# A written-out cyclic order for the head pairs of an attention and feed-forward kernel

## Chip, cores and metric

The kernel runs on one core of a Trainium2 chip. The metric is the device time of one execution in microseconds; before the change the median of three runs is 488.45 us (487.97 to 488.66).

## What is computed

Attention with a bias that depends on positions, over batch 4, 8 heads, 576 positions, head size 64, and then a gated feed-forward layer with a convolution over positions (hidden size 1024):

```python
scores = scale * np.matmul(q, k.transpose(0, 1, 3, 2))
x = (psi_rel / psi_i)[..., None]
h = np.maximum(x @ w1 + b1, 0.0)
bias = h @ w2
scores = scores + bias.transpose(2, 0, 1)[None, :, :, :]
attn = np.exp(scores - np.max(scores, axis=-1, keepdims=True))
attn = attn / (np.sum(attn, axis=-1, keepdims=True) + 1e-09)
attn_out = np.matmul(attn, v)
x = attn_out.transpose(0, 2, 1, 3).reshape(B, S, H * D)
h = np.maximum(x @ w_in, 0.0)
conv_out = sum(conv_w[k] * hp[:, k:k + S, :] for k in range(3))
out = (h * sigmoid(conv_out)) @ w_out
```

## The kernel before

**Stages.** First the bias of all heads is computed and written to a DRAM tensor `bias_d`; then comes the attention; then the feed-forward layer, one batch entry after another. The change is about the attention.

**Pairs and units.** Two heads of one batch entry are a head pair. There are 16 (`seq`, pairs 0 to 15: four batch entries for each of four positions `p` of a pair among the heads). A pair's query rows are split into five units: unit 0 holds 64 rows of each of the two heads in one tile of 128 (the "short unit": one reduction, one exponent), units 1 to 4 hold 128 rows of each head, one head after the other.

**A unit's work.**
- `scores` (L371): TensorE multiplies queries and keys into a PSUM tile `s`; there are two such tiles (`psS`). Each product has two matmul instructions and each head two column halves. One instruction group of a unit has 8 matmuls.
- `reduce` (L382): VectorE adds the bias tile `bt`, writes the result to `sp` in SBUF and takes the row minimum. It frees the `s` tile. There are three `sp` tiles, used in turn.
- `expo` (L396): ScalarE takes the exponent in place and the row sum.
- `side_transposes` (L430) and `transposes` (L442): TensorE turns the result in pieces of 64 rows, the last 64 key columns into free columns of a score tile (the side), the rest into two of three PSUM tiles `tp`.
- copies (`act` L101 on ScalarE, `dve` L104 on VectorE) bring the turned pieces to `ptx` (units 0 to 2, 320 columns) and `pty` (units 3 and 4, 256 columns).
- `pv_parts` (L479): the value products, five parts for each of the two groups, into the one PSUM tile `o`; then ScalarE copies `o` to `x` (also L101).

**Sums.** `invert` (VectorE) takes the reciprocals of a pair's row sums, `sum_transposes` or the second half of `side_transposes` (L434) turns them, a copy brings them to `rt`, `store_sums` (L506, L507) writes them to a DRAM tensor, `spread_sums` (L512) loads them back to all partitions as `rb`, and `apply_norm` (L519) multiplies `x` by them on GpSimd.

**Weights.** The feed-forward weights come as 28 narrowing jobs: SP loads a piece (`load_w`), VectorE shifts (L110), ScalarE converts (L112), VectorE merges (L116), and GpSimd splits the result in two parts (L144, L145). Bias tiles of the next `p` are fetched by DMAs on GpSimd's queue (`load_bias`) in the pairs of the last batch entry.

**The order.** Each engine works through its instructions in the order of the program; waits are set by tiles. The attention is one loop over `flat`, the list of units. Round `u` issues the scores and reductions of unit `u + 2`, the side transposes of unit `u`, the exponents of unit `u + 1`, the main transposes and copies of unit `u`, and then some value products from the queue `fill`, by a fixed share:

```python
pv_share = (2, 2, 1, 3, 2)
```

A narrowing job starts in every second round, with one step after the transposes and one after the value products. The sums of pair `n - 1` are inverted, turned, stored and loaded during pair `n`, and pair `n - 2` is multiplied in the middle of pair `n`.

Of the kernel before, what the change touches and what calls it, by code (L numbers as in the profile page):

```python
# [19 lines left out]
def attention_ffn_kernel(  # L20
# [87 lines left out]
    def narrow_steps(w, u, raw):  # L108

        nc.vector.tensor_scalar(w, raw[:, :, 0], 29, None, op0=ALU.logical_shift_right)  # L110
        yield
# [36 lines left out]
    with tc.manual_schedule():  # L148
# [190 lines left out]
        def new_sp(n, t):  # L339
            tag = len(nms) % SPB  # L340
# [85 lines left out]
        def side_transposes(side, n, t, sums):  # L426

            spf = spt[n, t][0]
            for a, ra in enumerate(halves_):
                tr = nc.tensor.transpose(side[:, a, HS:HS + TL].bitcast(F32R), spf[ra, 8 * P:9 * P], identr[ra, ra])  # L430
                after_exp(tr, n, t)
            if sums is not None:
                for a, ra in enumerate(halves_):
                    nc.tensor.transpose(side[:, a, HS + TL:HS + P], rr_t[sums % 2][ra], ident[ra, ra])  # L434

        def transposes(n, t, side=None, sums=None):
# [8 lines left out]
            v3 = [x.rearrange("p (s x) -> p s x", x=TL) for x in ps]  # L445
            (d0, c0), (d1, c1) = (place(n, t, a if t else 0) for a in range(2))
            if t:
                dve(halves(d0[:, 8, c0:c0 + P]), side[:, :, HS:HS + TL])
                if sums is not None:
                    rts[sums] = r_p.tile([9, P], F32, name="rt")  # L450
                    dve(halves(rts[sums]), side[0:9, :, HS + TL:HS + P])
# [11 lines left out]
        def pv_parts(n, g):  # L463
            p, b = seq[n]
# [4 lines left out]
            def part(c):  # L469
# [13 lines left out]
                if c == 4:  # L483
                    del ptt[n, g]
                    waiting[n] -= 1
                    if b not in xb:
                        xb[b] = x_p.tile([P, NP, S], F32, name=f"x{b}", tag="x")
                    act(xb[b][:, p, x0:x0 + width], po[:, 0:width])

            return [lambda c=c: part(c) for c in range(5)]  # L490

# [24 lines left out]
        def apply_norm(n):  # L516
            p, b = seq[n]
            assert waiting[n] == 0
            nc.gpsimd.tensor_mul(xb[b][:, p], xb[b][:, p], rbs.pop(n))  # L519
# [90 lines left out]
        conv_weights = {68: load_conv, 71: narrow_conv, 73: turn_conv}  # L610
# [7 lines left out]
        NU = len(flat)  # L618
# [6 lines left out]
        def unit_steps(n, t):  # L625
# [10 lines left out]
            if t:  # L636
                side = psE.tile([P, 2, 512], F32, name="s")
                side_transposes(side, n, t, None)
            transposes(n, t, side)
# [48 lines left out]
        pv_share = (2, 2, 1, 3, 2)  # L688
        hs_ff = {}
        raw_w = {}  # L690
        job_steps = iter(())
# [3 lines left out]
        for u, (n, t) in enumerate(flat):  # L695
            p, b = seq[n]
            ui = units.index(t)
            sums = n - 1 if ui == (2 if n > 1 else 3) and n else None
            side = None
            if u + 2 < NU:  # L700
                for h in heads(flat[u + 2][1]):
                    if side is not None:
                        reduce(side, *flat[u + 2], 0)
                    side = scores(*flat[u + 2], h)
            if t:
                if side is None:
                    side = psS.tile([P, 2, 512], F32, name="s")
                side_transposes(side, n, t, sums)
            if u + 2 < NU:
                reduce(side, *flat[u + 2], h)  # L710
            if u + 1 < NU:
                for h in heads(flat[u + 1][1]):
                    expo(*flat[u + 1], h)
                turned_sp(*flat[u + 1])
            while fill and u == 5:
                fill.popleft()()
            transposes(n, t, side, sums)
            next(job_steps, None)

            parts = len(fill) if u < 5 else pv_share[ui]  # L720
            while fill and parts > 0:
                fill.popleft()()
                parts -= 1
            next(job_steps, None)
            del spt[n, t]
            if u + 2 >= NU:
                f = u + 2 - NU
                ffn_in(0, f)
            if u in (2, 4) or n > 1 and ui == 2 and n + 2 < NSEQ:
                load(n + 2 if n > 1 else 2 + u // 4)  # L730
            if u in conv_weights:
                conv_weights[u]()

            for at, do in ((u - 7, "load"), (u - 11, "split")):
                job = at // 2
                if at % 2 == 0 or not 0 <= job < 4 * KC + 2 * FE:
                    continue
                if job < 4 * KC:
                    src, dst = w_in[job // 4 * P:job // 4 * P + P], wi[job // 4]
                else:  # L740
                    src, dst = w_out[(job - 4 * KC) // 2 * P:(job - 4 * KC) // 2 * P + P], wo[(job - 4 * KC) // 2]
                cs = slice(job % 4 * 256, job % 4 * 256 + 256) if job < 4 * KC else slice(job % 2 * 256, job % 2 * 256 + 256)
                if do == "load":
                    raw_w[job] = (e_p if job % 3 else woe_p).tile([P, 256, 2], I32, name="raw_w", tag="h")
                    load_w(raw_w[job], src[:, cs])
                else:
# [262 lines left out]
```

## Time and profile before

| | |
|---|---|
| median of the runs | 488.45 us |
| the profiled execution's own time | 488.07 us |
| span in its profile | 486.3 us |
| TensorE, matmuls in flight | 470.2 us, 97% |
| TensorE, weight loads | 332.5 us, 68% |
| VectorE | 358.7 us, 74% |
| ScalarE | 301.9 us, 62% |
| GpSimd | 148.0 us, 30% |
| chain that ended last | TensorE 90%, ScalarE 4%, DMA 3% |

The span is from the first to the last instruction; the execution's own time is 1.8 us longer. A busy share is the union of an engine's instructions over the span. Matmuls are pipelined and their ends are modelled, so 97% does not say that TensorE is at its peak. The bias stage ends near 60 us, the attention near 291, the feed-forward layer fills the rest.

### The profile page before, as it was taken

How to read it: one execution, taken by the hardware profiler on the slowest of the kernel's cores; microseconds unless marked ns; L12 is line 12 of the kernel's file. 1: busy time of each engine (PE TensorE's matmuls, PEld its weight loads, DVE VectorE, ACT ScalarE, POOL GpSimd, SP SyncE). 2: the span in 40 equal slices, each digit the busy share in tenths (PEclk: the TensorE clock that was granted, in tenths of full speed). 3: DMA queues.
4: the chain of work that ended last, by engine and by line, in shares of the span. 5: the costliest groups of instructions: out<-in, count | busy, mean ns of one | idle time of the engine just before them, and what ended most of it. 6: DMA issues, size and time to landing. Idle time of an engine off the chain costs nothing.

```text
span 486.3 us, 10561 instructions
## 1 busy us (share of the span) xinstructions
PE 470.2 (97%) x3914; PEld 332.5 (68%) x3914; DVE 358.7 (74%) x876; ACT 301.9 (62%) x711; POOL 148.0 (30%) x221
## 2 busy tenths in 40 slices
PE   5978899999999999999999999999999999999996
PEld 3332366666666666666666668988888888888886
DVE  6999976788888889988887821594489238936971
ACT  6998886787777778777778722682264126424530
POOL 1000001354555725467267728006000600060000
PEclk9999999999999999999999999999999999999999
DMA  1899857588668796689952300000100200020003
GB/s 48 235 350 297 339 155 170 137 261 219 167 173 208 192 264 148 176 213 252 243 132 60 113 26 25 1 2 11 75 1 0 88 22 1 0 86 2 0 1 108
DMA packets 32582, 60.79 MB, mean 125 GB/s; under 512 B 7196, under 2 KB 15796, under 8 KB 32532
## 3 DMA queue, kind: packets, MB, share of 16 engines
q1 hardware_dynamic: 27380, 47.02, 34.3%
q0 software_dynamic: 4768, 12.77, 9.6%
q8 instruction: 31, 0.51, 0.4%
q10 hardware_dynamic: 384, 0.35, 0.2%
q14 instruction: 19, 0.16, 0.1%
HBM read 44.12 MB, written 15.98 MB: 124 GB/s over the span
## 4 chain that ended last, share of the span: by engine, by line
PE 90%; ACT 4%; DMA 3%; DVE 1%; issue 1%; DVEq 0%; SPq 0%
PE s L555 20%; PE o L479 18%; PE s L371 17%; PE tp L827 16%; PE tp L442 9%; PE o L827 4%; PE s L278 4%; DMA bias_d<-st 2%; ACT st L304 1%; ACT y L257 1%; PE s L430 1%; DVE sp L382 1%; ACT tl L304 1%; DMA bt<-bias_d 1%; DMA pars<-in_par_dram 1%
## 5 line engine op out<-in xcount | busy, mean ns | idle before, releaser
L382 DVE CUSTOM_DVE_ANT_0 sp<-s,bt 128x576 f32<-128x576 f32 x144 | 104.1, 754 | 33.3 <-PE s L371 20.9
L396 ACT ACTIVATE sp<-sp,nm 128x576 f32<-128x576 f32 x144 | 110.0, 768 | 0.0
L371 PE MATMUL s<-qk 64*128 64x288 f32 (+1 forms) x640 | 93.3, 431 | 3.4 <-DVE nm L382 2.6
L555 PE MATMUL s<-xs,wi 128*128 128x512 f32 x384 | 88.6, 390 | 0.0
L555 PEld LDWEIGHTS s<-xs,wi 128*128 128x128 f32 x384 | 71.8, 188 | 15.8 <-DVE pty L104 0.5
L371 PEld LDWEIGHTS s<-qk 64*128 64x128 f32 (+1 forms) x640 | 46.7, 175 | 45.3 <-DVE nm L382 14.9
L827 PE MATMUL tp<-wo,g 128*128 128x512 f32 x288 | 70.3, 389 | 0.0
L442 PE MATMUL tp<-identr,sr 64*128 64x64 f32 x1184 | 64.6, 248 | 1.4 <-ACT sp L396 1.4
L802 DVE SCALAR_TENSOR_TENSOR cv<-h,cw,cv 128x575 f32<-128x575 f32 x64 | 52.4, 818 | 16.7 <-ACT cv L797 14.8
L827 PEld LDWEIGHTS tp<-wo,g 128*128 128x128 f32 x288 | 54.0, 188 | 11.2
L442 PEld LDWEIGHTS tp<-identr,sr 64*128 64x128 f32 x1184 | 55.8, 136 | 7.6 <-ACT sp L396 2.1
L568 ACT ACTIVATE h<-s 128x512 f32<-128x512 f32 x32 | 19.1, 598 | 57.5 <-PE s L555 57.5
L261 DVE TENSOR_SCALAR y<-tl,inv,nb 128x576 f32<-128x576 f32 (+33 forms) x112 | 47.6, 499 | 0.0
L479 PE MATMUL o<-ptx,vt 128*64 128x320 f32 x300 | 46.8, 442 | 0.2 <-issue 0.2
L479 PE MATMUL o<-pty,vt 128*64 128x256 f32 x320 | 44.2, 393 | 0.0
L278 PE MATMUL s<-y,pars 128*32 128x512 f32 (+8 forms) x352 | 42.1, 500 | 1.8 <-DVE y L261 1.0
L144 POOL TENSOR_SCALAR xs<-x 128x512 fp32r<-128x512 f32 (+1 forms) x16 | 11.2, 701 | 105.5 <-DVE gt L822 105.5
L506 POOL DMA_DIRECT2D r_d<-rt x16 | 10.0, 627 | 87.2 <-DVE rt L104 87.2
L101 ACT ACTIVATE ptx<-tp 128x256 f32<-128x256 f32 (+1 forms) x64 | 26.7, 443 | 14.4 <-PE tp L442 14.2
L808 ACT ACTIVATE cv<-cv 128x576 f32<-128x576 f32 x32 | 21.9, 684 | 21.9 <-DVE cv L802 21.8
L809 DVE SCALAR_TENSOR_TENSOR cv<-cv,h 128x576 f32<-128x576 f32 x32 | 24.1, 753 | 14.0 <-ACT cv L808 14.0
L101 ACT ACTIVATE pty<-tp 128x512 f32<-128x512 f32 x32 | 19.0, 592 | 23.2 <-PE tp L442 23.2
(91 smaller groups left out, 646.3 us busy)
## 6 DMA issues: line engine op xcount, KB each, us to landing
qk<-in_qk_dram SPq DMA_DIRECT2D x32, 320.0 KB, 6.1
bias_d<-st SPq DMA_DIRECT2D x13, 607.0 KB, 6.0
bt<-bias_d POOLq DMA_DIRECT2D x24, 288.0 KB, 7.1
qk<-in_qk_dram SPq DMA_DIRECT2D x32, 144.0 KB, 6.2
rb<-r_d POOLq DMA_DIRECT2D x32, 144.0 KB, 3.1
vt<-in_v_dram SPq DMA_DIRECT2D x16, 256.0 KB, 7.1
raw_w<-in_moe_w_in_dram SPq DMA_DIRECT2D x16, 256.0 KB, 5.2
out_dram<-o SPq DMA_DIRECT2D x16, 256.0 KB, 2.0
```

The lines of the kernel that those rows point to most:

```text
L101: nc.scalar.activation(o, i, AF.Copy)
L261: nc.vector.tensor_scalar(y, dist[:, 0:n], inv[:, ig:ig + 1], nb1, op0=ALU.mult, op1=ALU.max)
L278: nc.tensor.matmul(ps[32 * j:32 * j + 32, a // 512 if n > 512 else blk % 2, 0:min(n - a, 512)], w2b, ys[j][:, a:min(n, a + 512)], start=Tr ...
L371: nc.tensor.matmul(ps[po, a, 0:HS], qt[rows, qo:qo + po.stop - po.start], qt[rows, KO + hh * HS:KO + hh * HS + HS], start=True, stop=True,)
L382: nc.vector.tensor_tensor_reduce(out=halves(spt[n, t][0][:, h]), in0=ps[:, :, 0:HS], in1=halves(bt[:, h]), op0=ALU.add, op1=ALU.min, scale ...
L396: exps[n, t, h] = nc.scalar.activation(sp[:, h], sp[:, h], AF.Exp, bias=nm[:, h:h + 1], scale=-1.0, accum_out=sms[n][:, col:col + 1],)
L442: tr = nc.tensor.transpose(ps[a][:, TL * s:TL * s + TL].bitcast(F32R), spf[ra, j:j + P], identr[ra, ra])
L479: nc.tensor.matmul(po[D * h:D * h + D, 0:width], vt[:, slot, :], pt[:, blk, :], start=(c == 0), stop=(c == 4),)
L555: nc.tensor.matmul(ps, wi[c][:, pw, f * P:f * P + P], rhs(c, px), start=(i == 0), stop=(i == 3 * KC - 1))
L802: nc.vector.scalar_tensor_tensor(out=cv[:, o:o + S - 1], in0=h[:, i:i + S - 1], scalar=cw[:, f, kk:kk + 1], in1=cv[:, o:o + S - 1], op0=AL ...
L809: nc.vector.scalar_tensor_tensor(out=cv, in0=cv, scalar=1.0, in1=h, op0=ALU.add, op1=ALU.mult)
L827: nc.tensor.matmul(ps, lhs(f, gi), wo[f][:, wj, cs], start=(f == 0 and i == 0), stop=(f == FC - 1 and i == 2),)
```

## The change

The loop over `flat` keeps only its first seven rounds (pairs 0 and 1). Pairs 2 to 15 run through a table `CYCLE` of operations, each with a unit, a pair relative to the current one, and an engine. The table's letters: `S` scores, `R` reduce, `E` exponent, `T` main transposes, `s` side transposes, `k0`, `k1`, `k0b`, `k1b`, `c` copies, `P` value product parts, `xb` the copy of `o`, `inv`, `sm`, `rt`, `st`, `sp`, `AN` the steps of the sums, `J1` to `J3` and `W` the steps of a narrowing job. The engine `A` or `V` of a copy is written in the table. `st` stands with the pair before the current one, `sp` with the one before that, `AN` with the third before.

`per_pair` gives the jobs of each pair; pairs 3, 7 and 11, which fetch bias tiles, have none. A job's load is issued three jobs ahead. The turn of the convolution weights moves from rounds 68 to 73 to rounds 1 to 6. Side transposes get their own columns of the latest score tile (`side_cols`).

```diff
@@
-        for u, (n, t) in enumerate(flat):
...
+        for u, (n, t) in enumerate(flat[:7]):
...
+            if u in (1, 4, 6):
+                (load_conv, narrow_conv, turn_conv)[u // 3]()
...
+        NJ = 4 * KC + 2 * FE
+        per_pair = [0, 0, 3, 0, 2, 3, 3, 0, 2, 3, 3, 0, 3, 2, 2, 2]
...
+        def job_step(j, k):
+            if k == 1:
+                _, dst, cs = job_slices(j)
+                jobs[j] = split_w_steps(e_p, dst[:, :, cs], raw_w.pop(j), ("cv", "cv"))
+            ins = next(jobs[j])
+            if k == 1 and j in first_job:
+                shifts[first_job[j]] = ins
+            if k == 2:
+                load_job(j + 3)
...
+        CYCLE = """
+            S:2,0,0:P S:2,1,0:P T:0,0:P inv:-1:V P:1,0,-1:P P:1,1,-1:P R:2,0,0:V E:1,0,0:A S:3,0,0:P E:1,1,0:A
...
+        """.split()
...
+        def side_cols():
+            if now[0] is None or used[0] + TL > 512:
+                now[0], used[0] = psS.tile([P, 2, 512], F32, name="s"), HS
+            used[0] += TL
+            return now[0][:, :, used[0] - TL:used[0]]
...
+            elif k == "AN":
+                mul = apply_norm(n)
+                if shifts:
+                    tc.add_manual_dep(mul.ins, shifts.pop(max(shifts)).ins.name, DATA)
+                if n == NSEQ - B:
+                    x_parts(0, NP - 1)
...
+        for m in range(1, NSEQ + 1):
+            if m == NSEQ:
+                ffn_in(0, 1)
+            for entry in CYCLE:
...
+                if at[-1] == NSEQ:
+                    instead(op)
+                elif at[-1] < NSEQ and (at[-1] > 1 or op in late) and op not in begun and op not in tail:
+                    emit(op, dve if eng == "V" else act)
+                    begun.add(op)
```

In the last pair `instead` puts feed-forward products where the next pair's scores would stand.

What the table makes of TensorE's order: the rows below are of the middle of the attention, before the change, from the scores of unit 2 of a pair to the value products of unit 2's round (L371 scores, L430 side transposes, L434 the sums, L442 main transposes, L479 value products; rows of one tile name are drawn together).

```order
L371 MATMUL s<-qk 128x288 x4
L442 MATMUL tp<-identr,sr_59 128x64 x10
L479 MATMUL o<-pty,vt_119 64x256 x4
L371 MATMUL s<-qk 128x288 x4
L430 MATMUL s<-identr,sr_60 128x64 x2
L442 MATMUL tp<-identr,sr_60 128x64 x16
L479 MATMUL o<-pty,vt_119 64x256 x4
L371 MATMUL s<-qk 128x288 x4
L430 MATMUL s<-identr,sr_58 128x64 x2
L434 MATMUL s<-ident,rr_161 128x64 x2
L442 MATMUL tp<-identr,sr_58 128x64 x16
L479 MATMUL o<-pty,vt_119 64x256 x2
```

The changed kernel at the same place, from the scores of unit 2 to those of the next pair's unit 0 (L370, L429, L434, L442, L483 are the same lines):

```order
L370 MATMUL s<-qk 128x288 x4
L442 MATMUL tp<-identr,sr_58 128x64 x10
L483 MATMUL o<-pty,vt_118 64x256 x4
L370 MATMUL s<-qk 128x288 x4
L442 MATMUL tp<-identr,sr_59 128x64 x16
L370 MATMUL s<-qk 128x288 x2
L429 MATMUL s<-identr,sr_59 128x64 x2
L370 MATMUL s<-qk 128x288 x2
L442 MATMUL tp<-identr,sr_60 128x64 x16
L434 MATMUL s<-ident,rr_160 128x64 x2
L429 MATMUL s<-identr,sr_60 128x64 x2
L370 MATMUL s<-qk 64x288 x4
```

Before, value products stand after the transposes of every unit. Now unit 1's main transposes are followed by scores, its side transposes stand between the two heads of unit 4's scores, and unit 2's transposes are followed by the next pair's unit 0. The value products of the second group stand in two blocks and those of the first in one block of five parts at the end of the cycle.

ScalarE before, from the copy of the 320 value columns of a pair (L101 copies, L396 exponents, L112 a narrowing step):

```order
L101 ACTIVATE x_938<-o 128x320
L396 ACTIVATE sp_57,sm<-sp_57,nm 128x576 x2
L101 ACTIVATE ptx<-tp 128x4x64
L101 ACTIVATE ptx<-tp 64x64
L112 ACTIVATE wu<-raw_w 128x256
L396 ACTIVATE sp_55,sm<-sp_55,nm 128x576 x2
L101 ACTIVATE ptx<-tp 128x8x64
```

And now, from the same copy to the first big copy of the next pair (L395 exponents, L111 a narrowing step):

```order
L101 ACTIVATE x_133<-o 128x320
L395 ACTIVATE sp_56,sm<-sp_56,nm 128x576 x2
L101 ACTIVATE ptx<-tp 64x64 x2
L395 ACTIVATE sp_57,sm<-sp_57,nm 128x576
L101 ACTIVATE ptx<-tp 128x4x64
L111 ACTIVATE wu<-raw_w 128x256
L395 ACTIVATE sp_57,sm<-sp_57,nm 128x576
L101 ACTIVATE ptx<-tp 128x8x64
```

The copy of the value columns stood in the middle of a pair's second round of value products; now it stands between the last work of one pair and the exponents of unit 1 of the next, and a second 64x64 copy has come from VectorE.

## Rows read from the trace of the kernel before

**Rows 1.** Windows, twelve pairs: PE, PEld, DVE, ACT, POOL busy; clock; DMA.

```profile
97.99:269.23 171.24, 171.24 (x1970) 113.26 (x1968) 147.62 (x430) 132.59 (x340) 95.10 (x149) 1.00 0.75 191
```

**Rows 2.** Timeline of PE, one pair: start, us, engine, line, what.

```profile
157.50 1.24 PE L371 MATMUL s<-qk 64*128 64x288 f32 x8
158.36 0.41 PE L430 MATMUL s<-identr,sr 64*128 64x64 f32 x2
...
159.35 1.08 PE L479 MATMUL o<-pty,vt 128*64 128x256 f32 x8
160.36 1.24 PE L371 MATMUL s<-qk 64*128 64x288 f32 x8
161.22 0.41 PE L430 MATMUL s<-identr,sr 64*128 64x64 f32 x2
...
162.28 0.65 PE L479 MATMUL o<-pty,vt 128*64 128x256 f32 x4
162.86 0.72 PE L371 MATMUL s<-qk 64*64 64x288 f32 x8
163.51 0.25 PE L430 MATMUL s<-identr,sr 64*128 64x64 f32 x2
...
171.75 0.51 PE L371 MATMUL s<-qk 64*128 64x288 f32 x2
```

**Rows 3.** Timeline of PE near the attention's start.

```profile
80.95 0.83 PE L442 MATMUL tp<-identr,sr 64*128 64x64 f32 x16
81.62 1.23 PE L371 MATMUL s<-qk 64*128 64x288 f32 x8
82.48 0.41 PE L430 MATMUL s<-identr,sr 64*128 64x64 f32 x2
...
83.37 0.75 PE L371 MATMUL s<-qk 64*128 64x288 f32 x4
```

**Rows 4.** Timeline of PE, a whole group of value products of 320 columns.

```profile
74.86 2.91 PE L479 MATMUL o<-ptx,vt 128*64 128x320 f32 x20
77.70 0.69 PE L371 MATMUL s<-qk 64*64 64x288 f32 x5
```

**Rows 5.** Timelines of PE, DVE and PEld: scores, reductions, a waiting weight load.

```profile
151.88 1.24 PE L371 MATMUL s<-qk 64*128 64x288 f32 x8
152.69 0.76 DVE L382 CUSTOM_DVE_ANT_0 sp<-s,bt 128x576 f32<-128x576 f32 x1 [1.12 <-PE s L371]
...
48.97 0.76 DVE L382 CUSTOM_DVE_ANT_0 sp<-s,bt 128x576 f32<-128x576 f32 x1 [0.43 <-DMA bt<-bias_d]
49.65 0.08 DVE L382 DVE_READ_ACCUMULATOR2_ANT nm<- 128x1 f32 x1
...
49.78 0.30 PEld L371 LDWEIGHTS s<-qk 64*128 64x128 f32 x4 [2.51 <-DVE nm L382]
```

**Rows 6.** Timeline of ACT, back-to-back operations.

```profile
155.11 0.44 ACT L101 ACTIVATE x<-o 128x320 f32<-128x320 f32 x1 [0.68 <-PE o L479]
155.44 0.43 ACT L112 ACTIVATE wu<-raw_w 128x256 f32<-128x256 f32 x1
155.77 0.77 ACT L396 ACTIVATE sp<-sp,nm 128x576 f32<-128x576 f32 x1
...
156.53 0.76 ACT L396 ACTIVATE sp<-sp,nm 128x576 f32<-128x576 f32 x1
...
157.28 0.47 ACT L101 ACTIVATE ptx<-tp 128x256 f32<-128x256 f32 x2
```

**Rows 7.** Timelines of DVE and POOL: a first narrowing step, alone and beside GpSimd.

```profile
154.85 0.28 DVE L110 TENSOR_SCALAR wu<-raw_w 128x256 int32<-128x256 int32 x1
...
160.76 0.74 POOL L145 TENSOR_TENSOR wi<-wu,wi 128x256 fp32r<-128x256 f32 x1
160.89 0.76 DVE L110 TENSOR_SCALAR wu<-raw_w 128x256 int32<-128x256 int32 x1
```

More of the change, by code (lines that the diff above doesn't have):

```diff
@@ L484, in part, with pv_out @@
                     del ptt[n, g]
[L485 to L488, printed above, removed]
+                    if out:
+                        pv_out(n, g, act)
             return [lambda c=c: part(c) for c in range(5)]
+        def pv_out(n, g, copy):
+            p, b = seq[n]
+            x0, width = (XW, YW) if g else (0, XW)
+            waiting[n] -= 1
+            if b not in xb:
+                xb[b] = x_p.tile([P, NP, S], F32, name=f"x{b}", tag="x")
+            copy(xb[b][:, p, x0:x0 + width], ops_t.pop((n, g))[:, 0:width])
         def invert(n):
@@ L694, in attention_ffn_kernel @@
         wo = [wo01[:, f] for f in range(2)] + [woe_p.tile([P, 2, DM], F32R, name=f"wo{f}") for f in range(2, FE)]
-        for u, (n, t) in enumerate(flat):
-            p, b = seq[n]
-            ui = units.index(t)
-            sums = n - 1 if ui == (2 if n > 1 else 3) and n else None
+        for u, (n, t) in enumerate(flat[:7]):
+            sums = 0 if (n, t) == (1, 3) else None
             side = None
[L700 to L704, printed above, removed]
-            if t:
[L706 to L714, printed above, removed]
+            for h in heads(flat[u + 2][1]):
+                if side is not None:
+                    reduce(side, *flat[u + 2], 0)
+                side = scores(*flat[u + 2], h)
+            cols = [side[:, :, HS + i * TL:HS + i * TL + TL] for i in range(2)]
+            if t:
+                side_transposes(cols[0], n, t)
+            if sums is not None:
+                sum_transposes(cols[1], sums)
+            reduce(side, *flat[u + 2], h)
+            for h in heads(flat[u + 1][1]):
+                expo(*flat[u + 1], h)
+            turned_sp(*flat[u + 1])
@@ L715, in attention_ffn_kernel @@
             while fill and u == 5:
                 fill.popleft()()
[L717 to L721, printed above, removed]
+            place_all(transposes(n, t), n, t, cols[0], sums, cols[1])
+            while fill:
                 fill.popleft()()
-                parts -= 1
-            next(job_steps, None)
             del spt[n, t]
-            if u + 2 >= NU:
-                f = u + 2 - NU
-                ffn_in(0, f)
@@ L729, in attention_ffn_kernel @@
[L729 to L739, printed above, removed]
-                else:
[L741 to L746, printed above, removed]
-                    job_steps = split_w_steps(e_p, dst[:, :, cs], raw_w.pop(job), ("cv", "cv"))
@@ new lines, in attention_ffn_kernel @@
+        jobs, tiles, turned, side_of, sum_in, parts_of = {}, {}, {}, {}, {}, {}
+        now, used = [None], [0]
+        left, shifts = {}, {}
+        def job_step(j, k):
[7 more added lines that the diff above has]
+                load_job(j + 3)
@@ new lines, in after_turn, with instead @@
+        def after_turn(n, t):
+            if n == NSEQ - 2 and t > 1:
+                x_parts(0, t - 2)
+            if n == NSEQ - 1 and t in (1, 2):
+                load_wo(FE - 1 + t)
+        ahead = {}
+        def instead(op):
+            if op == ("S", 1, 0, NSEQ):
+                ahead[0] = psS.tile([P, 2, 512], F32, name="s")
+                main_products(ahead[0], 0, 0)
+            elif op[0] == "S":
+                now[0] = None
+            if op == ("E", 0, 0, NSEQ):
+                main_out(ahead[0], 0, 0)
```

174 lines of the change are left out of this document (126 added, 48 removed).

## The prediction

> **What bounds the kernel now.** I read the windows first. From 97.99 to 269.23 us, twelve head pairs, TensorE has a matmul in flight for 171.24 of 171.24 us at a granted clock of 1.00; VectorE is busy 147.62 and ScalarE 132.59 [rows 1]. Busy time alone proves little, since matmuls overlap, so the timeline of one pair comes next [rows 2]: the scores of one unit start at 157.50 and the same unit's of the next pair at 171.75, so a pair takes 14.25 us, and twelve take 171.24, or 14.27 each [rows 1]. No matmul row in between shows idle time in front of it. The starts within a pair show what fills it: TensorE goes round scores, transposes, value products once per unit, and each group takes a fixed time from its start to the next group's.
>
> The weight loads take 113.26 of the 171.24 us [rows 1], that is 66%. The Trainium skill ("Perfetto Trace Analysis", Identifying the Most-Contended Engine) calls matmul busy time a bad measure and judges TensorE's headroom by weight-load share; by that a third of the engine would be free and a wait elsewhere would set the pair. The trace bears this out only as rival 3 below: the same spacing pair after pair is what an engine limited by its own order looks like.
>
> **The price of a pair, by groups.** From start to next start, in the old order [rows 2]: scores of two heads 0.86 (157.50 to 158.36); side and main transposes, 18 instructions, 0.99 when value products follow; eight value products of 256 columns 1.01, four of them 0.58, so four more cost 0.43; 20 transposes 1.06; the scores of the short unit 0.65 (162.86 to 163.51). After scores, 18 transposes followed by scores instead of value products take 0.89 (82.48 to 83.37), and 16 transposes between value products and scores take 0.67 (80.95 to 81.62) [rows 3]: two transposes cost 0.083, and the step from transposes to scores is 0.10 cheaper than the step to value products. A whole group of 20 value products of 320 columns takes 2.84 (74.86 to 77.70) [rows 4], once instead of twice.
>
> **The change, part by part.** The matmuls are the same; the stops at value products fall from five in a pair to three. The new order, with those prices:
> scores of unit 2, 0.86; ten transposes of unit 0, 0.99 less four times 0.083, 0.66; eight value products 1.01; scores 0.86; 16 transposes followed by scores, 0.89 less 0.08, 0.81; scores of unit 4 with two side transposes between its heads; 20 transposes before the short unit, 1.06; the short unit 0.65; twelve value products 1.01 + 0.43 = 1.44; 16 transposes 0.67; scores 0.86; 20 transposes 1.06; the 20 value products 2.84.
> No row shows scores, two transposes, scores. It costs 0.86 if the two vanish behind the scores and 0.86 + 0.22 = 1.08 at most (0.22 is 0.89 less eight steps of 0.083); I take the middle, 0.97. Nor is there a row of transposes before the short unit: 0.96 if the step costs what it costs before scores, 1.06 as before value products; I take 1.06, since the short unit, like the value products, writes half of the partitions at a time. The short unit before value products is taken at its price before transposes.
> The sum is 13.75 us.
>
> **The new wait.** Only two score tiles exist, so the second head of unit 4 must wait until VectorE has reduced the second head of unit 3, with one group of transposes between instead of a whole unit. A reduction starts 0.81 after its scores group (151.88 to 152.69), the next one 0.68 later (48.97 to 49.65), and the weight load that was waiting comes 0.81 after the start of the reduction that frees its tile (48.97 to 49.78) [rows 5]. With unit 3's scores at 0.86 + 0.66 + 1.01 = 2.53, the reductions start at 3.34 and 4.02 and free their tiles at 4.15 and 4.83. Unit 4 wants them at 4.20 and about 4.80. The first is in time by 0.05; the second makes TensorE wait some 0.06 with the matmul's own start. So the pair takes **13.81**, and saves 14.25 - 13.81 = **0.44**.
>
> **The rest costs nothing while its cover holds.**
> - Copies change engines: the sums' copy and one big copy leave VectorE for ScalarE. VectorE is at 147.62 of 171.24 and gets lighter. ScalarE, 132.59 in twelve pairs, is 11.0 a pair and has 13.81.
> - ScalarE has one tight chain. The copy of the 320 value columns now stands ahead of the next pair's exponents, and waits for the last of the 20 value products: about 13.81 + 0.14, at 13.95. Behind it come four exponents, three small copies, a narrowing step and a big copy, which the transposes of unit 2 wait for, at 13.81 + 5.23 = 19.04. By the rows: the value copy 0.33 (155.11 to 155.44), the narrowing step 0.33, an exponent 0.76, two small copies 0.47 [rows 6]; in all 0.33 + 3.04 + 0.55 + 0.33 + 0.60 (a big copy, estimated from the small ones' rate) = 4.85, so 18.80, with 0.06 to release it 18.86. It is in time by some 0.2. Without the narrowing step it has 0.5.
> - The sums are stored, loaded and multiplied a pair or more later, so GpSimd's two waits on DMA get longer cover; nobody but the last multiplication is waited for.
> - 28 narrowing jobs stay 28; those moved out of the pairs that fetch bias tiles leave GpSimd's queue to the fetches there. Their loads stand three jobs ahead on SP's queue, behind the next pair's queries.
> - The turn of the convolution weights goes from the end of the attention to its start: the same transpose, no gain.
>
> **Sum.** Pairs 2 to 14 run whole cycles; the last pair has the same groups with feed-forward products in place of the next pair's scores, and I give it the same 0.44. 14 x 0.44 = 6.2. The profiled execution took 488.07 (its span is 486.3), so 481.9; the median of the runs, 488.45, stands 0.38 above it: **482.3**. The two open prices move it. With both cheap ends the wait of unit 4 still decides there, and only the 0.10 of the short unit is won: 13.71, 480.9. With the dear end of the split scores the wait vanishes in it: 13.86, 483.0.
>
> **Rivals.**
> 1. **GpSimd's port.** A first narrowing step took 0.28 alone (154.85), and 0.76 when it started beside a GpSimd subtraction of 0.74 (160.89 against 160.76) [rows 7]: 0.48 more. In the new order the second job of a pair starts just where the first job's split or the multiplication runs. VectorE has some 0.4 to spare before the last reduction of the cycle delays the next scores. If a job's step is held in most of the eleven pairs that have jobs, about 0.3 each remains on TensorE's path, 3.3 in all: 485.6. The Trainium skill ("SBUF — State Buffer", Who interferes with whom) has the shared port as an exclusive lock held for the whole instruction; this case's rows agree, and by that rule the multiplication, the longest of them, would hold a step longest.
> 2. **ScalarE becomes the bound: slower.** The chain above closes on itself: value products, value copy, four exponents, big copy, transposes of unit 2, value products. It decides once its eleven operations take 0.2 more. It loses what was won at 0.64 more, 0.06 an operation, and at 0.09 each (1.0) the pair takes 14.61, 0.36 over the old one: 14 x 0.36 = 5.0, 493.5. For it: no row has these operations back to back in this order. Against: each price above is from back-to-back rows.
> 3. **TensorE's order was not the bound**, or the savings are met by new waits of their size: 488.4. Against: the even spacing of [rows 2].
> 4. **The change gains more.** Both open prices are at their cheap ends and the reductions come early enough not to decide: 13.75 - 0.11 - 0.10 = 13.54, 0.71 a pair, 478.5; halfway from the forecast, 480.4. Against: VectorE's 0.81 and 0.68 are the same in every row I saw.
>
> **How the numbers follow.** Forecast (481 to 484) 0.52; rival 1 (484 to 487.4) 0.20; rival 4 0.11; rival 3 0.08; rival 2 0.09. A measurement of this kernel tells 0.2%, about 1 us, from no change. Faster is forecast, rivals 1 and 4: 0.83; same 0.08; slower 0.09. The range that leaves out rivals 2 and 3 and the far ends of the others is 479.8 to 486.8.
>
> **What would show it.** The scores of unit 2 should come every 13.8 us; eight value products, scores, 16 transposes, scores should stand in the timeline with the prices above; a weight load of the second head of unit 4 should show a short wait for VectorE. Wrong would be: a wait of transposes for ScalarE in each pair (rival 2), a narrowing step of 0.7 or more with scores waiting after it (rival 1), or the groups' prices themselves, if a step from transposes to scores costs as much as one through value products.

## The result, and the profile after

The changed kernel took **483.12 us** (median of 4, 482.75 to 485.34) beside 488.56 us of the kernel before in the same comparison: 0.99 of its time, 95% interval 0.9869 to 0.9932. The forecast was 482.3, so the gain is there and 0.8 us of it are missing in the medians. The profiled execution took 483.41 us; the prediction's sum for it was 481.9, so 1.5 us are missing there.

The page of the changed kernel: its first line, busy time by engine, and the chain that ended last, by engine.

```profile
span 481.5 us, 10562 instructions
PE 464.8 (97%) x3914; PEld 333.7 (69%) x3914; DVE 347.4 (72%) x834; ACT 312.9 (65%) x753; POOL 147.7 (31%) x221
...
PE 84%; DVE 7%; ACT 3%; DMA 3%; issue 1%; SPq 0%; DVEq 0%
```

As the copies moved, VectorE got 11.3 us lighter and ScalarE 11.0 us heavier. TensorE has 6 points less of the chain than before, and VectorE has 7% of it instead of 1%. Most of that is not the attention's: 21 us of VectorE's part lie before 66 us, 15 of them on L260 of the bias stage, where the chain took another path than before. From 98 to 250 us VectorE has none of the chain, in pairs 14 and 15 some 11 us: there are the new waits.

The windows, from the scores of unit 2 of pair 3 to those of pair 15, twelve pairs as in [rows 1] (columns as there).

```profile
97.99:264.59 166.60, 165.96 (x1970) 114.02 (x1968) 135.99 (x386) 140.26 (x371) 88.27 (x135) 1.00 0.74 189
```

The same 1970 matmuls take 166.60 us instead of 171.24, at the same granted clock of 1.00. They are no longer without a hole: 0.64 us have no matmul in flight.

The timeline of PE, one pair, to be read beside [rows 2].

```profile
97.99 1.24 PE L370 MATMUL s<-qk 64*128 64x288 f32 x8
98.85 0.72 PE L442 MATMUL tp<-identr,sr 64*128 64x64 f32 x10
99.50 1.08 PE L483 MATMUL o<-pty,vt 128*64 128x256 f32 x8
100.52 1.24 PE L370 MATMUL s<-qk 64*128 64x288 f32 x8
101.38 0.99 PE L442 MATMUL tp<-identr,sr 64*128 64x64 f32 x16
102.18 0.77 PE L370 MATMUL s<-qk 64*128 64x288 f32 x4
...
103.19 0.98 PE L442 MATMUL tp<-identr,sr 64*128 64x64 f32 x16
...
104.25 0.72 PE L370 MATMUL s<-qk 64*64 64x288 f32 x8
104.89 1.52 PE L483 MATMUL o<-pty,vt 128*64 128x256 f32 x12
106.34 0.83 PE L442 MATMUL tp<-identr,sr 64*128 64x64 f32 x16
107.01 1.24 PE L370 MATMUL s<-qk 64*128 64x288 f32 x8
...
108.95 2.91 PE L483 MATMUL o<-ptx,vt 128*64 128x320 f32 x20
111.79 0.51 PE L370 MATMUL s<-qk 64*128 64x288 f32 x2
```

From 97.99 to 111.79 a pair takes 13.80 us, and so do ten of the eleven from pair 3 to 13, within 0.02; pair 11 takes 13.89, because its short unit's scores come 0.08 late. **Pair 14 takes 14.65.** One more place is late: in pair 15, TensorE is at the end of the attention 21.30 us after the scores of unit 2 (264.59 to 285.90), before it was 21.45, a gain of 0.15 only. (In the two further traces of the changed kernel, below, pair 15 takes 21.00 and 21.01.)

The timelines of POOL, DVE and PE at the wait of pair 14.

```profile
258.54 1.42 POOL L529 TENSOR_TENSOR x<-x,rb 128x576 f32<-128x576 f32 x1
258.61 1.62 DVE L115 SCALAR_TENSOR_TENSOR wu<-wu 128x256 int32<-128x256 int32 x1
...
260.16 0.68 DVE L104 COPY ptx<-tp 128x512 f32<-128x512 f32 x1
...
260.89 0.34 PE L442 MATMUL tp<-identr,sr 64*128 64x64 f32 x4 [0.64 <-DVE ptx L104]
```

A last narrowing step takes 0.41 to 0.43 us in the pairs from 3 to 13. Here it starts 0.07 behind the start of GpSimd's multiplication by the inverted sums and takes 1.62. The copy of a transposed piece stands behind it on VectorE, and the transposes wait for the buffer that this copy frees: the 0.64 us without a matmul.

The same timelines at the wait of pair 15.

```profile
269.86 1.42 POOL L529 TENSOR_TENSOR x<-x,rb 128x576 f32<-128x576 f32 x1 [2.09 <-DVE wu L115]
270.50 0.93 DVE L110 TENSOR_SCALAR wu<-raw_w 128x256 int32<-128x256 int32 x1
...
272.23 0.68 DVE L104 COPY ptx<-tp 128x512 f32<-128x512 f32 x1
...
273.05 0.47 PE L442 MATMUL tp<-identr,sr 64*128 64x64 f32 x7 [0.50 <-DVE ptx L104]
```

Here it is a first narrowing step (0.29 alone), and the transposes wait 0.50. They also ask earlier than in a whole cycle: the last pair has no short unit of a next pair, 0.65 us of scores, in front of them.

**Where the time went.** The scores of unit 2 of pair 2 start 0.52 later than before (83.89 and 83.37). Of this 0.27 comes from the bias stage, which ended later in this execution (the same scores of pair 1 start at 66.44 and 66.17). The other 0.25 is the turn of the convolution weights, which now stands right in front of these scores. The timelines of PE at the turn, before and after.

```profile
274.63 0.24 PE L600 MATMUL tp<-ident,w 24*128 24x24 f32 x1
...
83.72 0.24 PE L610 MATMUL tp<-ident,w 24*128 24x24 f32 x1
```

With the turn between them, it is 0.91 from the transposes to the scores (82.98 to 83.89); without it, before, 0.65 (82.72 to 83.37). At its old place, in pair 15, the turn took 0.17 (274.63 to 274.80). Pair 2 gave 0.52 (14.62 to 14.10), pairs 3 to 14 gave 4.64 (171.24 to 166.60), pair 15 gave 0.15. Less the later start that is 4.79 at the first feed-forward product behind the attention (290.69 and 285.90), and still 4.79 at the start of TensorE's last matmul (482.16 and 477.37): the feed-forward layer passes it on whole. The two executions' own times differ by 4.66.

### The profile page after: what moved, and what is told of

The parts are those of the page before. It is cut to its first block, busy times and chain, and to the rows that moved or that the text cites. A ratio compares the mean times of both kernels' runs of the same rounds, so it can differ in the third digit from the quotient of the medians.

```text
span 481.5 us, 10562 instructions
## 1 busy us (share of the span) xinstructions
PE 464.8 (97%) x3914; PEld 333.7 (69%) x3914; DVE 347.4 (72%) x834; ACT 312.9 (65%) x753; POOL 147.7 (31%) x221
## 4 chain that ended last, share of the span: by engine, by line
PE 84%; DVE 7%; ACT 3%; DMA 3%; issue 1%; SPq 0%; DVEq 0%
PE s L565 21%; PE o L483 16%; PE tp L949 16%; PE s L370 15%; PE tp L442 9%; PE o L949 5%; DVE y L260 3%; DVE sp L381 2%; DMA bias_d<-st 2%; PE s L277 1%; ACT y L256 1%; ACT st L303 1%; DVE ptx L104 1%; DMA pars<-in_par_dram 1%; PE s L429 1%
## 5 line engine op out<-in xcount | busy, mean ns | idle before, releaser
L381 DVE CUSTOM_DVE_ANT_0 sp<-s,bt 128x576 f32<-128x576 f32 x144 | 105.5, 751 | 21.6 <-PE s L370 19.4
L395 ACT ACTIVATE sp<-sp,nm 128x576 f32<-128x576 f32 x144 | 110.4, 769 | 0.6 <-DVE nm L381 0.6
L370 PE MATMUL s<-qk 64*128 64x288 f32 (+1 forms) x640 | 94.9, 435 | 2.9 <-DVE nm L381 2.3
L442 PE MATMUL tp<-identr,sr 64*128 64x64 f32 x1184 | 69.3, 255 | 3.0 <-ACT sp L395 1.8
L442 PEld LDWEIGHTS tp<-identr,sr 64*128 64x128 f32 x1184 | 57.8, 136 | 17.4 <-ACT rt L101 3.8
L370 PEld LDWEIGHTS s<-qk 64*128 64x128 f32 (+1 forms) x640 | 45.7, 174 | 29.0 <-PE o L483 6.4
L260 DVE TENSOR_SCALAR y<-tl,inv,nb 128x576 f32<-128x576 f32 (+33 forms) x112 | 47.6, 500 | 0.0
L483 PE MATMUL o<-ptx,vt 128*64 128x320 f32 x300 | 43.7, 437 | 0.0
L483 PE MATMUL o<-pty,vt 128*64 128x256 f32 x320 | 41.2, 389 | 0.0
L101 ACT ACTIVATE pty<-tp 128x512 f32<-128x512 f32 x46 | 26.5, 595 | 19.4 <-PE tp L442 18.5
L277 PEld LDWEIGHTS s<-y,pars 128*32 128x32 f32 x352 | 15.5, 113 | 26.1 <-DVE y L260 11.4
```

The lines of the kernel that those rows point to most:

```text
L101: nc.scalar.activation(o, i, AF.Copy)
L260: nc.vector.tensor_scalar(y, dist[:, 0:n], inv[:, ig:ig + 1], nb1, op0=ALU.mult, op1=ALU.max)
L277: nc.tensor.matmul(ps[32 * j:32 * j + 32, a // 512 if n > 512 else blk % 2, 0:min(n - a, 512)], w2b, ys[j][:, a:min(n, a + 512)], start=Tr ...
L370: nc.tensor.matmul(ps[po, a, 0:HS], qt[rows, qo:qo + po.stop - po.start], qt[rows, KO + hh * HS:KO + hh * HS + HS], start=True, stop=True,)
L381: nc.vector.tensor_tensor_reduce(out=halves(spt[n, t][0][:, h]), in0=ps[:, :, 0:HS], in1=halves(bt[:, h]), op0=ALU.add, op1=ALU.min, scale ...
L395: exps[n, t, h] = nc.scalar.activation(sp[:, h], sp[:, h], AF.Exp, bias=nm[:, h:h + 1], scale=-1.0, accum_out=sms[n][:, col:col + 1],)
```

## The experiments

My theory: TensorE's order sets the time of a pair, by the prices of its groups; the rest is hidden. The main rival: it is hidden only where no narrowing step of VectorE meets an instruction of GpSimd.

**The changed kernel again**, twice.

> The changed kernel itself, again, as the base for the other runs of this chip. Theory (TensorE's order of groups) and rivals alike: 482.5 to 483.5 us, twelve of thirteen whole cycles of 13.80 to 13.81 us, one cycle (pair 14) of about 14.65.

> The changed kernel once more, to stand beside the kernel with the two edits in pairs 13 to 15: 482.8 to 483.6 us by either theory.

483.21 us (483.07 to 484.85), ratio 0.9899 (0.988 to 0.9918), and 483.56 us (482.7 to 483.96), ratio 0.9902 (0.9886 to 0.9919). Both traces have the cycles of the first one, with pair 14 at 14.62; pair 11 is at 13.92 in the first of them and at 13.81 in the second. Pair 15 takes 21.00 and 21.01 instead of 21.30: its first narrowing step beside the multiplication takes 0.63 there, not 0.93. So 0.3 of the wait of pair 15 belongs to the one execution shown above.

**Five stops at value products, all else of the change kept.** The table of the cycle is written in the order of the old rounds, with the new engines for the copies, the new places of the sums and the new pairs for the jobs.

```diff
-            S:2,0,0:P S:2,1,0:P T:0,0:P inv:-1:V P:1,0,-1:P P:1,1,-1:P R:2,0,0:V E:1,0,0:A S:3,0,0:P E:1,1,0:A
...
+            S:2,0,0:P R:2,0,0:V S:2,1,0:P R:2,1,0:V E:1,0,0:A E:1,1,0:A T:0,0:P k1b:0,0:A k0b:0,0:A k0:0,0:V k1:0,0:A
+            J1:0,0:V P:1,0,-1:P P:1,1,-1:P J2:0,0:A inv:-1:V
+            S:3,0,0:P R:3,0,0:V S:3,1,0:P s:1,0:P R:3,1,0:V E:2,0,0:A E:2,1,0:A T:1,0:P c:1,0:V k0:1,0:A k1:1,0:A
+            J3:0,0:V P:1,2,-1:P P:1,3,-1:P W:0,0:G
...
```

> The table is written in the old order of rounds, with five stops at value products, and keeps everything else of the change: copies on the engines of the new table, sums stored, loaded and multiplied as late, jobs in the same pairs. Theory (TensorE's order is the whole gain): 14.25 a pair, 488.5 to 489.5 us, as before the change. Rival (lighter VectorE and later sums carry it): 483 to 485.

488.51 us (487.74 to 489.91), ratio 1.0 (0.999 to 1.0011): the time before. The timeline of PE, the short unit of two pairs in a row.

```profile
106.76 0.72 PE L370 MATMUL s<-qk 64*64 64x288 f32 x8
...
121.01 0.72 PE L370 MATMUL s<-qk 64*64 64x288 f32 x8
```

14.25 us, as in [rows 2]. With the old order of TensorE's groups, moving copies, sums and jobs gains nothing. The gain is the order's. (VectorE's and ScalarE's orders stand in the same table and follow the rounds too.) Why a stop costs what it costs was not taken apart: the prices are measured, not explained.

**Four stops**: one of the two stops that the change takes out is put back.

```diff
-            k1b:0,0:A k0b:0,0:A R:2,1,0:V S:3,1,0:P J1:0,0:V k0:0,0:V E:2,1,0:A T:1,0:P R:3,0,0:V S:4,0,0:P
+            k1b:0,0:A k0b:0,0:A R:2,1,0:V S:3,1,0:P J1:0,0:V k0:0,0:V E:2,1,0:A T:1,0:P P:1,2,-1:P R:3,0,0:V S:4,0,0:P
...
-            T:2,0:P E:3,1,0:A J1:2,0:V sm:-1:P s:2,0:P E:3,0,0:A k1:1,0:A S:0,0,1:P E:4,0,0:A P:1,2,-1:P
+            T:2,0:P E:3,1,0:A J1:2,0:V sm:-1:P s:2,0:P E:3,0,0:A k1:1,0:A S:0,0,1:P E:4,0,0:A
```

> One part of the value products moves in the table from the second block to behind unit 1's transposes: TensorE stops at value products four times a pair instead of three; nothing else moves. Theory (the pair's time is the sum of TensorE's group prices): 16 transposes before value products 0.91, four value products 0.58, less 0.81 and less 0.43, so 0.25 more, less the 0.05 that unit 4 then need not wait: 14.0 a pair, 14 pairs, 2.8 us, 485.9 us. Rival (the gain came from VectorE's lighter load and the later sums): 483.1.

494.07 us (492.33 to 497.38), ratio 1.0121 (1.008 to 1.0162): slower than the kernel before, and far from the 485.9 that I expected. The cycles are 14.14 to 14.16 us in some pairs, 0.15 above the 14.0 that the prices of groups give, and 14.98 or 14.99 in six (4, 5, 8, 9, 12 and 13). The timelines of POOL, DVE and PE in one of the six.

```profile
119.34 1.40 POOL L529 TENSOR_TENSOR x<-x,rb 128x576 f32<-128x576 f32 x1
119.53 1.37 DVE L110 TENSOR_SCALAR wu<-raw_w 128x256 int32<-128x256 int32 x1
...
121.70 0.67 DVE L104 COPY ptx<-tp 128x512 f32<-128x512 f32 x1
...
122.52 0.30 PE L442 MATMUL tp<-identr,sr 64*128 64x64 f32 x3 [0.75 <-DVE ptx L104]
```

In the new order of three stops the second job's first step starts beside a split of 0.74 us and takes 0.68 (at 117.70 us); moved by a stop, it starts beside the multiplication and takes 1.37.

The six cycles make 5.0 us. The profiled execution (497.38 us) loses more in pair 15, which takes 25.78: there, too, steps are held, transposes wait 1.96 us for a copy of VectorE, and right behind that the granted clock is 0.50 from 285 to 290 us, the lower of its two levels (1.2 GHz). Twelve feed-forward products take 5.49 us there, and 3.04 in the changed kernel.

**Four stops, the multiplication held behind that step.** It already waits for the first step of a pair's first job; now it waits for that of the second.

```diff
-        first_job = {sum(per_pair[0:n]): n for n in range(NSEQ) if per_pair[n]}
+        first_job = {sum(per_pair[0:n]) + 1: n for n in range(NSEQ) if per_pair[n]}
```

> The four-stop order of the last batch again, and the multiplication by the inverted sums on GpSimd now waits for the first step of the pair's second narrowing job instead of that of the first job; nothing else is moved. Theory (GpSimd's port): the 0.83 us that six of the four-stop cycles took beyond 14.15 us came from that step standing beside the multiplication (1.37 us, alone 0.29). It then falls back to 0.29 to 0.4 us, the six cycles to 14.15, and the run from 494.1 to 494.1 - 6 x 0.83 = 489.1 us (488.3 to 489.9). Rival (the four-stop order itself brings the copies late): the cycles stay at 14.98 and the run at 493.5 to 494.5.

488.41 us (487.46 to 494.79), ratio 0.9999 (0.9978 to 1.002): 5.7 us less, for one wait added on GpSimd. The same timelines.

```profile
119.39 0.29 DVE L110 TENSOR_SCALAR wu<-raw_w 128x256 int32<-128x256 int32 x1
119.76 1.42 POOL L529 TENSOR_TENSOR x<-x,rb 128x576 f32<-128x576 f32 x1 [0.52 <-DVE wu L110]
119.82 0.76 DVE L381 CUSTOM_DVE_ANT_0 sp<-s,bt 128x576 f32<-128x576 f32 x1
```

The step is at 0.29, five of the six cycles at 14.14 to 14.16 and one at 14.28, and the main rival's mechanism is shown: what cost 0.83 in each of six pairs, 5.0 us in all, was the order of two instructions on two engines. Pair 15 is shorter as well, 21.74. The last row is a reduction that starts inside the multiplication and still takes 0.76, as alone.

**Jobs in the pairs that fetch bias tiles.**

```diff
-        per_pair = [0, 0, 3, 0, 2, 3, 3, 0, 2, 3, 3, 0, 3, 2, 2, 2]
+        per_pair = [0, 0] + [2] * 14
```

> The changed kernel with two narrowing jobs in each of pairs 2 to 15, those that fetch bias tiles (3, 7, 11) too, instead of up to three in the others. Theory (TensorE's order sets the time, and VectorE has room in a bias pair as in any other): cycles stay at 13.80 to 13.82 and the run at 483.1 to 484.1 us. Rival (a job in a bias pair costs by VectorE's and the queues' extra work there): pairs 3, 7 and 11 are longer by 0.5 us or more each, and the run is at 484.6 us or more.

486.59 us (486.14 to 489.85), ratio 0.9965 (0.9944 to 0.9986): the rival's numbers came. Pairs 3, 7 and 11 take 14.70, 14.65 and 14.66, pair 14 again 14.66, the others 13.80 to 13.84. Pair 3, timelines of POOL, DVE and PE.

```profile
105.85 1.14 POOL L191 DMA_DIRECT2D bt<-bias_d  x2
...
106.89 1.83 DVE L115 SCALAR_TENSOR_TENSOR wu<-wu 128x256 int32<-128x256 int32 x1
107.00 1.43 POOL L529 TENSOR_TENSOR x<-x,rb 128x576 f32<-128x576 f32 x1
...
109.37 0.84 PE L442 MATMUL tp<-identr,sr 64*128 64x64 f32 x16 [0.72 <-DVE ptx L104]
```

The rival's reason is not in the rows: they show no wait for a queue. Issuing the bias fetches holds GpSimd until 106.99, and so puts the multiplication beside the last narrowing step, which takes 1.83. In pairs 7 and 11 the same step takes 1.77.

**No second job in pair 14, none in pair 15.**

```diff
-        per_pair = [0, 0, 3, 0, 2, 3, 3, 0, 2, 3, 3, 0, 3, 2, 2, 2]
+        per_pair = [0, 0, 3, 0, 3, 3, 3, 0, 3, 3, 3, 0, 3, 3, 1, 0]
```

> Pairs 14 and 15 keep one narrowing job and none instead of two each; pairs 4, 8 and 13 take three. Theory (in the last two pairs VectorE's narrowing steps are held by GpSimd, which there also splits the feed-forward input, and TensorE's transposes wait for the copies behind them, 0.84 and 0.66 us): pair 14 falls from 14.65 to 13.8, the wait in pair 15 goes, 481.6 us (481.2 to 482.2). Rival (the waits there come from the splits themselves or from the missing scores): no change, 483.1.

482.94 us (481.96 to 486.55), ratio 0.9879 (0.9862 to 0.9895). The 481.6 that I expected did not come. Pair 14 is at 13.82: its wait is gone. In pair 15 it is 0.37 from the first to the second transpose of the late group, and 0.74, 0.44 and 0.46 in the three traces of the changed kernel (two of them take 0.08 without a wait). So 0.29 of the wait stays without any job; that it is the missing short unit fits, but no run shows it alone. And pair 12 now takes 14.89. The timeline of PE there.

```profile
233.03 0.71 PE L370 MATMUL s<-qk 64*64 64x288 f32 x6 [0.38 <-DMA qk<-in_qk_dram]
```

The scores of the next pair's short unit wait for their queries and keys. That the jobs brought forward, two more by then, delay this load is my reading; no run took it apart. The trace is that of the slowest of the five executions (486.55 us), whose attention starts 3.3 us late, behind a bias stage with a granted clock of 0.73 from 50 to 60 us; whether pair 12 waits in the others is not shown.

**Pairs 13 to 15 mended another way**: in pair 14 the multiplication waits for the second job's last step, and one job moves from pair 15 to 13. It was measured twice.

```diff
...
-        per_pair = [0, 0, 3, 0, 2, 3, 3, 0, 2, 3, 3, 0, 3, 2, 2, 2]
+        per_pair = [0, 0, 3, 0, 2, 3, 3, 0, 2, 3, 3, 0, 3, 3, 2, 1]
...
+            if (k, j) == (3, sum(per_pair[:14]) + 1):
+                shifts[14] = ins
+                emit(("AN", 11), None)
...
```

> The changed kernel with two edits in pairs 13 to 15 alone: in pair 14 the multiplication by the inverted sums waits for the last step of the second narrowing job, so that the two do not run side by side; and one job of pair 15 is moved to pair 13. Theory (GpSimd's port): pair 14's last narrowing step falls from 1.62 to 0.42 us and its cycle from 14.65 to 13.81 (-0.84); pair 15's wait before its third group of transposes shrinks by 0.3 to 0.6; the run is at 483.2 - 1.1 to 1.4 = 481.8 to 482.1 us. Rival (those waits come from the splitting of the feed-forward input or from unit 4's second head, not from the step beside the multiplication): pair 14 stays above 14.4 and the run at 482.9 to 483.4 us.

> The kernel with the two edits in pairs 13 to 15 once more, in five rounds beside the changed kernel, because its first measurement (483.45 us, 482.29 to 484.59) did not tell it from the changed kernel's 483.2 although its trace shows pair 14 shorter by 0.76 us and pair 15's wait shorter by about 0.1 to 0.3. Theory (what the trace shows is whole in the time, and the rest was the bias stage's scatter from execution to execution): 0.7 to 1.1 us under the changed kernel in this call. Rival (something behind the attention gives it back): within 0.3 us of it.

483.45 us (482.29 to 484.59), ratio 0.9887 (0.9855 to 0.9919), then 483.24 (482.26 to 486.0), ratio 0.99 (0.9878 to 0.9922), beside 483.56 of the changed kernel: too near to tell apart, and neither the 481.8 to 482.1 of the first theory nor the 0.7 to 1.1 of the second came. In the traces pair 14 is at 13.89 and 13.92, pair 15 at 20.94 and 20.93. The timelines of DVE, PE and POOL in the first of the two (its line numbers are one lower).

```profile
260.10 0.69 POOL L142 TENSOR_SCALAR xs<-x 128x576 fp32r<-128x576 f32 x1
260.18 0.88 DVE L115 SCALAR_TENSOR_TENSOR wu<-wu 128x256 int32<-128x256 int32 x1
...
261.72 0.84 PE L441 MATMUL tp<-identr,sr 64*128 64x64 f32 x16
...
262.30 1.41 POOL L528 TENSOR_TENSOR x<-x,rb 128x576 f32<-128x576 f32 x1
```

Pair 14's second job stayed and only the multiplication moved: the cycle fell by 0.7. The step is still held, to 0.88, beside the split of a feed-forward input (L142) that took the multiplication's place. Of the 0.7 the second profiled execution lost 0.31 in pair 8, where the short unit's scores came late as in pair 11 above; in the first the attention's start-up stood 1.6 us later, as the bias stage did (the scores behind its large group at 79.57 instead of 77.95; the granted clock was 0.83 from 50 to 60 us). Such scatter is as large as what was to be measured.

**The sums one pair earlier**, as they were before the change.

```diff
-            P:1,3,-1:P P:1,4,-1:P R:4,1,0:V c:2,0:V rt:-1:A k0:2,0:V J2:2,0:A R:0,0,1:V E:4,1,0:A AN:-3:G
-            T:3,0:P S:1,0,1:P J3:2,0:V k1:2,0:V S:1,1,1:P k0:3,0:A xb:1,-1:A s:4,0:P T:4,0:P W:2,0:G sp:-2:G
+            P:1,3,-1:P P:1,4,-1:P R:4,1,0:V c:2,0:V rt:-1:A k0:2,0:V J2:2,0:A R:0,0,1:V E:4,1,0:A AN:-2:G
+            T:3,0:P S:1,0,1:P J3:2,0:V k1:2,0:V S:1,1,1:P k0:3,0:A xb:1,-1:A s:4,0:P T:4,0:P W:2,0:G
...
-            P:0,3,0:P P:0,4,0:P R:1,0,1:V k0:4,0:A E:0,0,1:A xb:0,0:A W:4,0:G c:4,0:V R:1,1,1:V
+            P:0,3,0:P P:0,4,0:P R:1,0,1:V k0:4,0:A E:0,0,1:A xb:0,0:A W:4,0:G sp:-1:G c:4,0:V R:1,1,1:V
...
```

> The changed kernel with the inverted sums loaded one pair earlier and their multiplication one pair earlier (two pairs behind the unit instead of three), and the split of the last input part behind it at the start of pair 15. Theory (the later sums are off TensorE's path; they only set which pair a multiplication falls in): 482.5 to 483.5 us, cycles at 13.80 to 13.82. Rival (the multiplication must be late, or GpSimd waits for the load with the split of a weight queued behind it): cycles at 14.0 or more, the run at 484 us or more.

493.83 us (490.68 to 496.98), ratio 1.0104 (1.0073 to 1.0135). My theory missed by 10 us. Cycles run from 13.81 to 16.08. The waits from pair 3 to 13 (engine, line, waited for: us in total, times, longest), and behind them the first two as the kernel before has them from 98 to 270 us.

```profile
POOL rb L522 <- DMA r_d<-rt: 42.5, 10, 9.5
POOL x L529 <- DMA rb<-r_d: 24.1, 6, 5.2
...
DVE sp L381 <- DMA bt<-bias_d: 8.6, 8, 2.7
...
POOL rb L512 <- DMA r_d<-rt: 36.4, 12, 6.2
POOL x L519 <- DMA rb<-r_d: 19.2, 5, 6.0
```

In the changed kernel's waits over the same pairs none of the three stands. GpSimd stops for the store of the sums to land, and for the load; the splits of the weights and the fetches of the bias tiles stand behind it, and the reductions wait for tiles. The two stops need not cost anything: the kernel before makes them too, nearly as long, and its reductions wait for no bias tile in these pairs. What else differs between the two orders was not taken apart. Some narrowing steps also meet the multiplication (1.32 us at 153.10). Which of the two edits, the earlier load or the earlier multiplication, does more wasn't tried: there is one buffer for the loaded sums.

**Two copies back on VectorE**: the big copy of unit 1 and that of the sums.

```diff
-            T:2,0:P E:3,1,0:A J1:2,0:V sm:-1:P s:2,0:P E:3,0,0:A k1:1,0:A S:0,0,1:P E:4,0,0:A P:1,2,-1:P
-            P:1,3,-1:P P:1,4,-1:P R:4,1,0:V c:2,0:V rt:-1:A k0:2,0:V J2:2,0:A R:0,0,1:V E:4,1,0:A AN:-3:G
+            T:2,0:P E:3,1,0:A J1:2,0:V sm:-1:P s:2,0:P E:3,0,0:A k1:1,0:V S:0,0,1:P E:4,0,0:A P:1,2,-1:P
+            P:1,3,-1:P P:1,4,-1:P R:4,1,0:V c:2,0:V rt:-1:V k0:2,0:V J2:2,0:A R:0,0,1:V E:4,1,0:A AN:-3:G
```

> The changed kernel with the big copy of unit 1 and the copy of the sums back on VectorE, as before the change. Theory (VectorE's slack in a pair with narrowing jobs is some 0.4 us and already spent on the step that the multiplication or a split holds; a big copy is 0.68 there): the last reductions of such a pair come late by about 0.3 us, cycles of the nine job pairs at 14.0 to 14.2 and the run at 485 to 487 us. Rival (VectorE has room for both copies, so moving them gained nothing): cycles at 13.80 to 13.82, the run at 483.0 to 483.6 us.

489.72 us (488.49 to 496.31), ratio 1.0032 (1.0013 to 1.0052): the whole gain is lost, more than I expected. From pair 3 to 13 the pairs with jobs take 14.40 to 14.42, and the bias pairs, which have none, 13.81 or 13.82. The timelines of DVE and PE, a pair with jobs.

```profile
121.13 0.68 DVE L104 COPY ptx<-tp 128x512 f32<-128x512 f32 x1
...
122.61 0.27 DVE L104 COPY rt<-s 9x128 f32<-9x128 f32 x1
122.81 0.67 DVE L104 COPY ptx<-tp 128x512 f32<-128x512 f32 x1
...
123.62 0.59 PE L442 MATMUL tp<-identr,sr 64*128 64x64 f32 x10 [0.39 <-DVE ptx L104]
```

The first two rows are the copies put back; the third is the copy that frees the buffer for the transposes of unit 3. VectorE has no room for them where a job runs.

The trace is of the longest execution (496.31 us). Its cycles are read before 281 us, at a granted clock of 1.00. Behind them pair 15 loses time as with four stops: transposes wait 1.48 and 1.45 us, and the granted clock is 0.50 from 285 to 290 us. The cycles of pairs 3 to 13 make 4.8 of the 6 us lost; how much pair 15 loses in the other executions is not shown.

## Why the prediction was right, and where it was off

- **The bound and the groups: right.** The pair was forecast at 13.81 and takes 13.80. Ten transposes took 0.65 (0.66 forecast), eight value products 1.02 (1.01), 16 transposes between scores 0.80 (0.81), twelve value products 1.45 (1.44), the large group 2.84. Of the two open prices, the 20 transposes before the short unit cost 1.06, the end I took. The split scores with two transposes cost 1.01 together with the wait; with four stops, where no wait is left, 0.97 (117.69 to 118.66 in the timeline), the middle I took. No term is off by more than 0.02, and what is off cancels; that the sum is right to 0.01 is partly luck. For four stops the same prices gave 14.0, and 14.15 came.
- **The wait of unit 4: right.** The timelines of DVE, ACT, PEld and PE in the pair that starts at 111.79:

```profile
114.32 1.24 PE L370 MATMUL s<-qk 64*128 64x288 f32 x8
...
115.12 0.76 DVE L381 CUSTOM_DVE_ANT_0 sp<-s,bt 128x576 f32<-128x576 f32 x1 [0.31 <-PE s L370]
...
115.81 0.75 DVE L381 CUSTOM_DVE_ANT_0 sp<-s,bt 128x576 f32<-128x576 f32 x1
...
116.37 0.58 ACT L101 ACTIVATE ptx<-tp 128x512 f32<-128x512 f32 x1
...
116.62 0.30 PEld L370 LDWEIGHTS s<-qk 64*128 64x128 f32 x4
...
117.00 0.64 PE L442 MATMUL tp<-identr,sr 64*128 64x64 f32 x8
```

  Scores at 114.32, reductions 0.80 and 0.69 later, the weight load 0.81 behind the second: the times of [rows 5]. The load's row names no releaser, so the times are the evidence, and the 0.04 by which the split scores are cheaper with four stops; 0.06 was forecast. So rival 4's cheaper pair did not come.
- **TensorE's headroom.** Matmuls in flight without a hole and weight loads at 66% spoke against each other [rows 1]. Five stops and three stops, with the same engines of the copies, places of the sums and jobs, differ by 5 us. The Trainium skill ("Perfetto Trace Analysis", Identifying the Most-Contended Engine) judges TensorE's headroom by the share of weight loads (and by how much arithmetic is done), and has the engine with the highest occupancy optimized first. By that it was VectorE's turn, with 147.62 of 171.24 us, and here the case disagrees: with five stops VectorE is busy 130.67 of 170.94 us in the same twelve pairs, and nothing is gained. On the headroom it does not disagree: the same matmuls went faster in another order. That a wait elsewhere would then set the pair was the prediction's own inference; as rival 3 it did not come.
- **ScalarE's chain: right that it does not decide, but its room was mis-sized.** The big copy ended 5.16 us into the pair (116.37 and 0.58 in the rows just shown), not 4.99; the transposes came at 5.21. So 0.05 was left of the 0.2: the step from the second exponent to the small copies took 0.88 instead of 0.76 (113.03 to 113.91), and the three small copies 0.61 instead of 0.55. (The chain also has ten operations by the prediction's own list, not eleven.) The pairs without jobs, where the narrowing step falls away, are not shorter, so rival 2 is out; that the miss stayed below 0.2 was luck.
- **What failed: "the last pair ... I give it the same 0.44", and 14 pairs at one price.** The term of 14 x 0.44 = 6.2 was mis-sized at its ends; between the two profiled executions 4.66 came. Pairs 3 to 14 gave 4.64 instead of 12 x 0.44 = 5.28, because pair 14 lost 0.84 (pair 11 lost 0.09; the kernel before had two longer pairs of its own, 14.37 and 14.44). Pair 2's gain of 0.52 went into the later start, half of it into the turn of the convolution weights, which the prediction had put at "no gain". Pair 15 gave 0.15 instead of 0.44, and the turn that left it is worth 0.17 alone. That is 0.64 + 0.44 + 0.29, and 0.13 stands outside the attention: the 1.5 that the sum lacks. In the two other traces of the changed kernel pair 15 gave 0.45 and 0.44, so the loss that stands in all three is pair 14's. Rival 1 was right in its mechanism and wrong in its place: it expected 0.3 in most pairs with jobs. There the second job's first step is indeed held, 0.67 or 0.68 instead of 0.29, and VectorE absorbs it. The 0.4 that VectorE had to spare stood in the prediction without a row; the runs show that a step held by 0.39 costs nothing, and that of the 0.94 us of the two copies put back 0.60 a pair came through. The meeting decides where a step meets the whole multiplication: in pair 14, and partly in 15.
- **"The rest costs nothing while its cover holds": right, but I did not ask how much cover.** In the old order the side edits together gain nothing. Taken back one at a time in the new order, the earlier sums cost 10 us, the copies 6, the jobs in bias pairs 3. In the last case I named the fetches' queue; the step beside the multiplication was the cause.

## What to carry to other kernels

When an engine's order is the bound, price a reordering by start-to-start times of its groups, taken from rows with the same neighbours; here the sum was right to 0.01 us for a pair with three stops, and 0.15 too low with four. Price the first and last rounds apart from the cycle. For every cover that a forecast leans on, write down its size: here 0.4 us on VectorE and one pair on GpSimd's queue were what stood between a gain of 5 us and a loss of 5.

## What I had not expected of the hardware

How sharp the meeting of VectorE and GpSimd is. A narrowing step of 0.29 or 0.42 us takes 1.35 to 1.83 when a multiplication of 1.40 to 1.43 starts within some 0.2 us of it, and less the later in the multiplication it starts: 0.93 at 270.50, 0.48 at 150.68 (beside one from 149.57 to 151.01). A start 0.55 us later on GpSimd gives all of it back (119.34 in the pair that starts at 112.94, and 119.76 in that of 112.81). Reductions and copies that read PSUM are not held: 0.73 to 0.76 and at most 0.69 us beside the multiplication. With jobs in the bias pairs the step began 0.05 to 0.11 before the multiplication by the rows, in three pairs, and was still the one held. The Trainium skill ("SBUF — State Buffer", Who interferes with whom) has an exclusive lock, taken by whoever issues first, for VectorE instructions in a two-port mode or with two SBUF inputs; the lengths agree (a held step ends 0.15 to 0.29 behind the multiplication), and so do the reductions, which have one SBUF input; a start that the rows put first does not show who holds the lock.
